# Windowed attention and a squared-relu MLP on one core: the last 512 tokens' first product by seven products, a longer lag of the second product, and a new set of planner constants

## The chip, the core and the metric

The kernel runs on one core of one Trainium2 chip. The metric is device time in microseconds (us). A core has a matrix engine (TensorE, PE in the profile, with its weight loads as PEld), three engines for elementwise work (VectorE is DVE, ScalarE is ACT, GpSimd is POOL) and a synchronisation engine (SP); DMAs are issued from the queues of SP, ACT and POOL. Matrix products land in PSUM, eight banks of 128 partitions x 512 float32; DVE and ACT carry them to SBUF. Each engine works through its own instructions in the order in which they were written, and waits on semaphores for the others.

## The reference, cut to what matters

```python
# q, k, v: (8, 8, 576, 64) = batch, heads, positions, head size; float32
scores = matmul(q, k.T) / sqrt(64)
scores = where(abs(pos_i - pos_j) <= 32, scores, -1e9)      # a band of 65 keys
attn   = softmax(scores)
x = matmul(attn, v), turned to (8*576, 8*64)                # 4608 tokens x 512
h = x @ w_in                                                # 512 -> 2048, "first product"
g = maximum(h, 0) ** 2
out = g @ w_out                                             # 2048 -> 512, "second product"
```

The output is 4608 x 512 float32. The two products are 4608 x 512 x 2048 multiplications each; they run in bf16 with float32 sums.

## The kernel before, in words

**Units.** The 4608 tokens are counted in 72 units of 64. Attention works on 24 groups G of 192 queries (three units, three groups to a batch element, all eight heads at once). The first product works on tiles of 192 tokens up to token 2304 and of 256 tokens after that (`TILES`). The second product works on blocks u of 128 tokens; blocks 0 and 1 are done directly (`mm2`), the others in 17 pairs (`PAIRS`, `mm2_pair`).

**Attention** (`scores_steps` L697, `pv` L753, `xturn`). q and k arrive in rows (`load_qk`, `load_pair`: DMAs on POOL's queue, with a conversion to bf16). They must be turned so that the head size lies on partitions: for groups 0 to 5 (`TG = 6`) by PE transposes (`turn_pe`, L568) and an eviction, later by transposing DMAs on SP's queue (`turn_dma`, L608). PE makes scores, ACT takes exp (L711, L714), DVE multiplies by the band's mask (L719, L725), PE multiplies by v with a column of ones beside it, DVE takes the reciprocal of the sums (L772) and scales (L775) into rows of x, xa (64 tokens) and xb (128 tokens). x must be turned as well: groups below `NXT` do it by PE transposes (L833, L838; group 0 by L808 and L803) and an eviction by ACT (L850), the others by two transposing DMAs on SP's queue (L854, L857) into `XT`.

**First product** (`mm1`, L879). For a tile and each column block of 128 of the 2048 columns, four matmuls with the weight block as the stationary side and the turned x as the moving side. A PSUM bank takes 512 elements (two column blocks of a 256-token tile). ACT takes the relu (L885), and DVE (L893) or ACT (L895) the square, into `GT`, a ring of 24 units.

**Second product** (`mm2_pair`, L965). Two blocks of 128 tokens x 2048 times 2048 x 512 are seen as a 2 x 2 by 2 x 2 block product and made by Winograd's form of Strassen's scheme: seven products where eight are the plain way. DVE forms four sums of `GT` blocks a pair (S1 to S4, L951); sums of the weights are formed once (`setup_tw`, L932). Each of the seven products is eight matmuls of 256 columns. The evictions: P1 goes to SBUF (L976 on ACT or L978 on DVE), DVE adds it to the next (L985: u2, u4, c22, cc), and the last two products accumulate in the bank. Every second pair from block `ULATE` on uses two of attention's banks, which are free by then.

**The order is planned.** Every instruction is recorded with the engine it may run on, a duration from a formula, what it reads and writes, and a key: its place in the work, in units. A list scheduler (`Prog.schedule`) then walks through the time: whenever an engine is free, it takes, of what is ready, the one with the lowest key. What comes out is a fixed order for each engine; nothing is decided on the chip. Attention of group G has the key 3G − `LEAD`, the first product of unit t has t + `MOE` (t − 1), the second product's pair at block u has 2u + `LAGP`. `OFFS` shifts the keys of single kinds of DVE and ACT work (S: the sums of the second product and so on), `FLEX` gives the handicap in units at which a kind may run on its second engine ('g': a square on ACT), `NOISE` and `SEEDS` shift all keys at random. The scheduler also plans the DMAs: a queue, a service time (`QMOVE`, `VMOVE`, `TMOVE`, ...), and then a slack, the time after which the planner counts the data as there: `LSLACK` for loads, `TSLACK` for turned q and k, `XSLACK` for turned rows of x. A load of group G from `GFAR` = 12 on is issued on POOL after a gate, the product with v of group G − 3.

Of the kernel before, what the change touches and what calls it, by code (L numbers as in the profile page):

```python
# [19 lines left out]
RING = 1536  # L20
NV, NRAW = 6, 6
TG = 6
NXT = 3
LEAD = 8
LAG = 9.0
AHEAD = 7
GFAR = 12
GATE = 'P{}B'
GD = 3
GK = 8.0  # L30
TDKEY = 6
XKEY = (0.2, 0.5)
QMOVE = 14.8
HMOVE = 27
PMOVE = 21.5
WMOVE = 86.0
VMOVE = 14.8
TISS = 1340
TMOVE = 12
TGAP = 28  # L40
NVR = 24
VKEY = 10.0
TSLACK = 3500
XSLACK = 2500
LSLACK = 3000
NCLR = 1
LANDQ = 2000
PQ = 100
# [17 lines left out]
SEEDS = (54889, 73113, 37345, 76131, 20885, 97248, 47624, 10448, 1997, 7471, 50773, 3305, 47783, 64133, 39018, 28670, 69087, 23028, 92194, 70005)  # L66
NOISE = 0.0
NBIAS = 1
PKEY = 2
MKEY = (-9.5, -6.5)  # L70
VSET = (-9.8, -6.8)
ESPLIT = 0
SDUR = 541
IOTA = -1
OPENING = [('k', 1), ('w1', 0), ('v', 0, 0), ('q', 1), ('v', 0, 1), ('q', 2), ('w1', 1), ('q', 5),
# [281 lines left out]
class Gen:  # L357
# [103 lines left out]

    def gate(self, G):
        if G < 6:
            return None
        return self.p.named[GATE.format(G - GD)] if G >= GFAR else self.moe

    def load_qk(self, t, b, g, key):
        t0, n = KC[g] if t == "k" else (192 * g, 192)  # L470
        h = n // 2
        G = 3 * b + g
        raw = self.RAW[t][G % NRAW]
        src = (self.q if t == "q" else self.k)[b]
        s = src[:, t0:t0 + n, :].rearrange("h (j p) d -> p j h d", j=2)
        for j in range(2):
            self.p.rec("POOL", lambda e, j=j: e.dma_start(raw[0:h, j, :].rearrange("p (h d) -> p h d", h=8), s[:, j]),  # L477
                       writes=[("raw", t, G % NRAW, j)], dma=(f"{t}{G % NRAW}{j}", G), key=key, dur=500 + 3 * h,
                       move=(h // 2, QMOVE), name=f"{t}{b}{g}{j}", after=self.gate(3 * b + g), slack=LSLACK if b > 1 else 0)

    def load_hw(self, t, g, key):

# [19 lines left out]
    def load_pair(self, t, b, g, key):  # L502

        t0, n = KC[g] if t == "k" else (192 * g, 192)
        h = n // 2
        G = 3 * b + g
        pr, raw = self.PR[t][G % NPR], self.RAW[t][G % NRAW]
        s = (self.q if t == "q" else self.k)[b][:, t0:t0 + n, :].rearrange("h (p r) d -> p h (r d)", r=2)
        self.p.rec("POOL", lambda e: e.dma_start(pr[0:h, :].rearrange("p (h c) -> p h c", c=128), s), writes=[("pr", t, G % NPR)],
                   dma=(f"{t}p{G % NPR}", G), key=key, dur=500 + 3 * h, move=(h // 2, PMOVE), name=f"{t}{b}{g}",  # L510
                   slack=LSLACK1 if b else 0)
        self.p.rec("DVE", lambda e: e.tensor_copy(raw[0:h, :, :].rearrange("p r (h d) -> p r h d", d=64),
                                                  pr[0:h, :].rearrange("p (h r d) -> p r h d", r=2, d=64)),
                   reads=[("pr", t, G % NPR)], writes=[("raw", t, G % NRAW, x) for x in range(2)], key=3 * G - LEAD - PKEY if b == 0 else key, dur=430,
                   name=f"c{t}{b}{g}")

    def load_v(self, b, g, key, js=(0, 1)):
        G = 3 * b + g
        vt = self.V[G % NV]
        for j in js:  # L520
            k0 = 192 * g - 32 + 128 * j
            lo, hi = max(k0, 0), min(k0 + 128, S_)
            if g and j == 0 and G < NVR:
                lo = k0 + 64
            n = hi - lo
            self.p.rec("POOL", lambda e, j=j, lo=lo, hi=hi, k0=k0: e.dma_start(  # L526
                vt[lo - k0:hi - k0, j, :, 0:64], self.v[b, :, lo:hi, :].rearrange("h p d -> p h d")),
                writes=[("v", G % NV, j)], dma=(f"v{G % NV}{j}", G), key=key, dur=500 + 3 * n, move=(n // 2, VMOVE),
                name=f"v{b}{g}{j}", after=self.gate(3 * b + g), slack=LSLACK if b > 1 else LSLACK1 * b)

    def copy_v(self, G, key):
# [86 lines left out]
    def scores(self, G, ws):  # L618
        b, g = divmod(G, 3)
        i = b % 2  # L620
        kt, qt = self.KT[i], self.QT[i]
        key = 3 * G - LEAD + 0.3 * ws[0]
        a = 192 * g
        reg = {w: w if len(ws) == 2 or G < NBIAS else 0 for w in ws}
        if G < NBIAS:
# [57 lines left out]
    def scores_steps(self, G):  # L683
        b, g = divmod(G, 3)
        i = b % 2
        kt, qt = self.KT[i], self.QT[i]
        key = 3 * G - LEAD
        a = 192 * g
        n = G % 2

# [38 lines left out]
    def pv(self, G, w):  # L729
        b, g = divmod(G, 3)  # L730
        n = 2 * G + w
        key = 3 * G - LEAD + 0.3 * w + 0.1
# [55 lines left out]

    def xturn(self, G):
        xa, xb = self.XA[G % 3], self.XB[G % 3]  # L790
        key = 3 * G - LEAD + 0.5
        r = 192 * G % RING
        wr = [("xt", (3 * G + c) % (RING // 64)) for c in range(3)]
        if G < NXT:
            ps = self.AT[:, 1024:1536].bitcast(BF16)
            bank = self.half(2)
# [65 lines left out]
    def mm1(self, t0, n, ds, key):  # L862
# [26 lines left out]
        if SQBEG <= t0 < SQEND and k % SQMOD[1] in SQMOD[0]:  # L889
# [4 lines left out]
                   reads=[("rt", k % 4)], writes=wr, key=key, dur=dve(c), name=f"g{t0}.{d0}",  # L894
                   alt=("ACT", lambda e: e.activation(gt[:, d0:d0 + len(ds), r:r + n], rr, ACTF.Square), act(c), "g")  # L895
                   if "g" in FLEX else None)

    def mm2(self, u, seg, key):
        op, gt = self.OUTP[u % 2], self.GT
# [158 lines left out]
    def build(self):  # L1058
# [40 lines left out]
        for G in range(NG):  # L1099
            b, g = divmod(G, 3)  # L1100
            if b > 1:
                key = 3 * G - LEAD - (GK if G >= GFAR else AHEAD)
                for t in "kq":
                    at(key, self.load_pair if G < TG else self.load_qk, t, b, g, key)
                at(key, self.load_v, b, g, key)
                if g and G < NVR:
                    key = 3 * G - LEAD - 0.5 if G >= VCS else key
                    at(key + 0.01, self.copy_v, G, key - VKEY if G >= VCS else key)
            for t in "kq":
                key = 3 * G - LEAD - (0.6 if G < TG else TDKEY)  # L1110
                at(key, self.turn_pe if G < TG else self.turn_dma, t, b, g, key)
            for ws in ((0,), (1,)) if G < NSPLIT else ():
                at(3 * G - LEAD + 0.3 * ws[0], self.scores, G, ws)
            if G >= NSPLIT:
                at(3 * G - LEAD, self.scores_steps, G)
            for w in range(2):
                at(3 * G - LEAD + 0.3 * w + 0.1, self.pv, G, w)
            at(3 * G - LEAD + 0.5, self.xturn, G)
# [62 lines left out]
```

## Time and profile before

| | |
|---|---|
| time, median of 3 runs | 290.84 us (290.55 to 291.35) |
| the profiled execution: its time, its span | 292.3 us, 290.1 us |
| granted TensorE clock, mean | 0.999 |
| busy: PE, PEld, DVE, ACT, POOL (us) | 283.0, 245.6, 208.2, 206.3, 107.0 |
| matmuls of the first product, L879 | 1248 to ht, 64 to outp, 32 to at |
| DMA, mean over the span | 138 GB/s, 39.97 MB |
| read and written in HBM | 36.70 MB, 9.44 MB |

The span runs from the first to the last instruction of the profiled execution; its time has what lies around it as well. Rows of groups give busy time and the mean of one instruction; a matmul's record is the time from its start to its modelled end, so that neighbours overlap, and how fast a stream of matmuls goes is better read from the chain of waits, which has starts and lengths of runs of them. The line numbers are those of the kernel before.

### The profile page before, as it was taken

What the parts mean: (1) busy time and instruction counts of PE and PEld (TensorE: products, weight loads), DVE (VectorE), ACT (ScalarE), POOL (GpSimd) and SP (SyncE); (2) the same over time, 40 slices, a digit from 0 to 9 for tenths busy, and PEclk for the clock granted to TensorE, in tenths of its full rate; (3) what the DMA queues carried; (4) which work ended last, traced back from release to release, by engine and by line L of the source; (5) the groups of instructions that cost most, each with busy time, mean ns of one, the idle gap of its engine ahead of it and who ended that gap; (6) DMA issues with size and microseconds to landing.
All of it is one profiled execution on the core that took longest, in us unless ns stands there. A gap on an engine that the chain in (4) does not pass through costs nothing.

```text
span 290.1 us, 8378 instructions
## 1 busy us (share of the span) xinstructions
PE 283.0 (98%) x3426; PEld 245.6 (85%) x3430; DVE 208.2 (72%) x451; ACT 206.3 (71%) x379; POOL 107.0 (37%) x143
## 2 busy tenths in 40 slices
PE   7988999999999999999999999999999999999996
PEld 2467885889999999999998898888888888988885
DVE  6668779878687878686968886766876877735263
ACT  3379987586989988778776677758687638688520
POOL 8986660141566066326415435606236000000000
PEclk9999999999999999999999999999999999999999
DMA  9999999999999999999999999999999921202024
GB/s 161 188 194 186 197 178 139 200 135 173 113 143 209 129 165 119 173 171 143 124 150 189 150 127 169 131 190 90 169 106 139 143 91 29 84 18 76 0 75 145
DMA packets 160645, 39.97 MB, mean 138 GB/s; under 512 B 149984, under 2 KB 156256, under 8 KB 160608
## 3 DMA queue, kind: packets, MB, share of 16 engines
q0 software_dynamic: 106016, 17.93, 94.2%
q1 hardware_dynamic: 49552, 12.47, 31.4%
q10 hardware_dynamic: 5040, 9.05, 9.8%
q8 instruction: 27, 0.44, 0.7%
q14 instruction: 10, 0.08, 0.1%
HBM read 36.70 MB, written 9.44 MB: 159 GB/s over the span
## 4 chain that ended last, share of the span: by engine, by line
PE 87%; DVE 6%; ACT 3%; DMA 1%; issue 1%; ACTq 0%; DVEq 0%
PE ht L879 39%; PE outp L965 29%; PE at L965 4%; PE at L753 4%; PE at L697 3%; PE outp L405 2%; DMA oe<-in_q_dram 1%; PE at L879 1%; PE outp L905 1%; PE outp L879 1%; DVE xa L775 1%; DVE tw L932 1%; ACT qt L596 1%; DVE kt L599 1%; ACT e L674 1%
## 5 line engine op out<-in xcount | busy, mean ns | idle before, releaser
L879 PE MATMUL ht<-xt,w 128*128 128x192 bf16 (+1 forms) x1248 | 135.9, 258 | 0.0
L879 PEld LDWEIGHTS ht<-xt,w 128*128 128x128 bf16 x1248 | 109.3, 98 | 7.9 <-ACT qt L596 0.3
L885 ACT ACTIVATE rt<-ht 128x384 bf16<-128x384 f32 (+1 forms) x156 | 82.4, 534 | 36.4 <-PE ht L879 31.4
L477 POOL DMA_DIRECT2D kraw<-in_k_dram x36 | 27.7, 775 | 113.1 <-PE at L753 54.6
L895 ACT ACTIVATE gt<-rt 128x384 bf16<-128x384 bf16 (+1 forms) x116 | 65.3, 569 | 4.4 <-ACT rt L885 1.5
L526 POOL DMA_DIRECT2D v<-in_v_dram x48 | 37.7, 793 | 0.0
L965 PE MATMUL outp<-w,gt 128*128 128x256 bf16 x240 | 31.1, 273 | 0.0
L965 PE MATMUL outp<-tw,gt 128*128 128x256 bf16 x240 | 31.1, 273 | 0.0
L965 PE MATMUL outp<-tw,ss 128*128 128x256 bf16 x240 | 30.5, 273 | 0.3 <-DVE ss L951 0.2
L893 DVE TENSOR_TENSOR gt<-rt 128x384 bf16<-128x384 bf16 (+1 forms) x52 | 19.9, 386 | 13.5 <-ACT rt L885 13.0
L477 POOL DMA_DIRECT2D qraw<-in_q_dram x36 | 27.7, 773 | 0.0
L711 ACT ACTIVATE e<-at 128x1024 bf16<-128x1024 f32 x21 | 21.4, 1020 | 7.3 <-PE at L697 7.0
L965 PEld LDWEIGHTS outp<-tw,ss 128*128 128x128 bf16 x240 | 22.9, 98 | 3.1 <-issue 0.3
L965 PEld LDWEIGHTS outp<-w,gt 128*128 128x128 bf16 x240 | 23.0, 98 | 3.0 <-ACT oe L915 0.5
L965 PEld LDWEIGHTS outp<-tw,gt 128*128 128x128 bf16 x240 | 22.9, 98 | 2.5
L985 DVE TENSOR_TENSOR oe<-outp,uu 128x256 f32<-128x256 f32 (+1 forms) x30 | 16.6, 554 | 8.2 <-ACT rt L885 4.9
L719 DVE TENSOR_TENSOR pt<-e,mask 128x1024 bf16<-128x1024 bf16 x21 | 14.5, 691 | 11.1 <-ACT e L711 11.0
L753 PE MATMUL at<-v,pt 128*128 128x66 bf16 x384 | 20.1, 194 | 0.1
L753 PEld LDWEIGHTS at<-v,pt 128*128 128x128 bf16 x384 | 17.8, 98 | 2.2 <-ACT at L783 0.4
L725 DVE TENSOR_TENSOR pt<-em,mask 64x512 bf16<-64x512 bf16 x42 | 17.6, 420 | 1.7 <-ACT em L714 0.3
L775 DVE TENSOR_TENSOR xa<-at,rs 64x512 bf16<-64x512 f32 x24 | 16.7, 695 | 1.1
L775 DVE TENSOR_TENSOR xb<-at,rs 128x512 bf16<-128x512 f32 x24 | 16.5, 686 | 0.8
(112 smaller groups left out, 321.8 us busy)
## 6 DMA issues: line engine op xcount, KB each, us to landing
out_dram<-oe ACTq DMA_DIRECT2D x34, 256.0 KB, 4.0
qraw<-in_q_dram POOLq DMA_DIRECT2D x36, 96.0 KB, 6.2
w<-in_moe_w_in_dram POOLq DMA_DIRECT2D x4, 512.0 KB, 11.1
v<-in_v_dram POOLq DMA_DIRECT2D x16, 128.0 KB, 7.8
w<-in_moe_w_out_dram POOLq DMA_DIRECT2D x4, 512.0 KB, 17.7
v<-in_v_dram POOLq DMA_DIRECT2D x16, 96.0 KB, 7.0
kraw<-in_k_dram POOLq DMA_DIRECT2D x12, 112.0 KB, 5.5
kraw<-in_k_dram POOLq DMA_DIRECT2D x12, 96.0 KB, 4.4
```

The lines of the kernel that those rows point to most:

```text
L477: self.p.rec("POOL", lambda e, j=j: e.dma_start(raw[0:h, j, :].rearrange("p (h d) -> p h d", h=8), s[:, j]), writes=[("raw", t, G % NRAW, ...
L526: self.p.rec("POOL", lambda e, j=j, lo=lo, hi=hi, k0=k0: e.dma_start(vt[lo - k0:hi - k0, j, :, 0:64], self.v[b, :, lo:hi, :].rearrange("h ...
L711: self.p.rec("ACT", lambda e: e.activation(e2[:], self.AT[:, 0:1024], ACTF.Exp, scale=0.125), reads=lo, writes=[("e", n)], key=key, dur=ac ...
L725: self.p.rec("DVE", lambda e, w=w, r=r, x=x, mm=mm: e.tensor_tensor(pt[x:x + 64, w, :, 0:64], e1[r:r + 64, :].rearrange("p (h q) -> p h q" ...
L753: mm = e.matmul(avp[:, c:c + VS], pt[:, 4 * (h % 2) + h // 2, :], vt[:, w, h, :], start=(w == 0 and y == 0), stop=True, skip_group_check=True)
L775: self.p.rec("DVE", lambda e: e.tensor_tensor(x[r0:128, :].rearrange("p (x y c) -> p x y c", x=2, y=4), av[:, :, :, 0:64], rb, ALU.mult), ...
L879: mm = e.matmul(ht[:, n * x:n * x + n], self.W1[:, ft, 128 * d:128 * d + 128], self.XT[:, ft, r:r + n], start=(ft == 0), stop=(ft == 3))
L885: self.p.rec("ACT", lambda e: e.activation(rt[:, 0:c], ht[:, 0:c], ACTF.Relu), reads=htag, writes=[("rt", k % 4)], key=key, dur=act(c), na ...
L893: self.p.rec("DVE", lambda e: e.tensor_tensor(gt[:, d0:d0 + len(ds), r:r + n], rr, rr, ALU.mult), reads=[("rt", k % 4)], writes=wr, key=ke ...
L895: alt=("ACT", lambda e: e.activation(gt[:, d0:d0 + len(ds), r:r + n], rr, ACTF.Square), act(c), "g")
L965: mm = e.matmul(op[:, 256 * half:256 * half + 256], a[:, d, :], w[:, d, :], start=first and d == 0, stop=d == 7, skip_group_check=True)
L985: self.p.rec("DVE", lambda e: e.tensor_tensor(out, src, other, ALU.add), reads=btags[bank] + rd, writes=wr, key=key + k * PSTEP - DLEAD, d ...
```

## The change

The first product of tokens 4096 to 4607, before two tiles of 256 tokens, is made as one tile of 512 in the manner of the second product: x as 2 x 2 blocks (halves of the 512 features, halves of the 512 tokens), the weights as 2 x 2 blocks (halves of the features, halves of the columns). `setup_w1s` forms four sums of weight blocks on DVE (eight instructions of 1024 elements), `mm1_tile` four differences of x blocks (512 elements), and `mm1_pair` runs, for each of eight pairs of column blocks (dd and dd + 8), seven products of two matmuls of 256 columns, an eviction (p1) and a relu on ACT, four additions on DVE, a relu of the other three quarters (DVE or ACT) and a square of 1024 elements (DVE or ACT). The buffers are those of finished work (raw q and k, `QT`, `KT`, `V`); pairs alternate between the two banks of `HT` and two banks of attention.

All else is constants, and a key of attention that runs ahead by 0.2 units a group after the sixth. `NXT` goes from 3 to 5, so the rows of x of groups 3 and 4 are turned on PE instead of by DMA; `TG` is 6 on both sides. `LAGP` goes from 8 to 14. Slack: `XSLACK` 2500 to 3200, `TSLACK` 3500 to 2200, `LSLACK` 3000 to 1200. The gate of loads is one group earlier.

```diff
-NXT = 3
+NXT = 5
-GK = 8.0
-TDKEY = 6
+GK = 7.0
+TDKEY = 5.0
 QMOVE = 14.8
+QM2 = 21.4
+TBK = 0
+GDL = 1
-TGAP = 28
+TGAP = 16
-TSLACK = 3500
-XSLACK = 2500
-LSLACK = 3000
+TSLACK = 2200
+XSLACK = 3200
+LSLACK = 1200
+STR1 = (4096,)
+LG0 = 6
+LGS = 0.2
+WLEAD = 3
-SEEDS = (54889, ...)
-NOISE = 0.0
+SEEDS = (43876, ...)
+NOISE = 0.1
-PKEY = 2
+PKEY = 0.2
-           ('k', 2), ('v', 1, 0), ('w1', 2), ('v', 1, 1), ('w1', 3), ('q', 3), ('v', 2, 0), ('v', 2, 1),
-           ('k', 3), ('v', 3, 0), ('w2', 2), ('v', 3, 1), ('w2', 0), ('w2', 1), ('hq', 0), ('v', 5, 1),
+           ('k', 2), ('v', 1, 0), ('w1', 2), ('v', 1, 1), ('w1', 3), ('q', 3), ('v', 2, 0), ('v', 3, 1),
+           ('v', 2, 1), ('k', 3), ('v', 3, 0), ('w2', 2), ('w2', 0), ('w2', 1), ('hq', 0), ('v', 5, 1),
-LAGP = 8.0
-PSTEP = 0.4
-SLEAD = 2.5
+LAGP = 14.0
+PSTEP = 0.35
+SLEAD = 1.0
-SQBEG = 768
-ULATE = 28
-HLATE = 4352
+SQBEG = 576
+ULATE = 26
+HLATE = 3840
-OFFS = {'S': 3.25, 'M': -1.5, 'g': 2.25, 'Z': -3.5, 'N': 2.75, 'cc.': -4.25, 'u': -2.75, 'X': 3.25, 'r': -2.25, 'c': -2.25}
+OFFS = {'S': 2.5, 'M': -2.5, 'g': 2.25, 'Z': 3.25, 'N': -1.75, 'cc.': -3.0, 'u': -2.0, 'X': -0.5, 'r': -2.25, 'c': -1.0}
-TWKEY = 6
+TWKEY = 7
-FLEX = {'g': 5.25, 'Z': 4.75, 'ev': 3.0, 'o': 6, 'p': 0.75}
+FLEX = {'g': -1.75, 'Z': -2, 'ev': 0.25, 'o': 4.75, 'p': 3.25, 'm': -1.5}
...
+    def pos(self, G):
+        return 3 * G - LEAD - max(0, G - LG0) * LGS
...
-        return self.p.named[GATE.format(G - GD)] if G >= GFAR else self.moe
+        return self.p.named[GATE.format(G - GD - GDL * (G > LG0))] if G >= GFAR else self.moe
...
-                       move=(h // 2, QMOVE), name=f"{t}{b}{g}{j}", after=self.gate(3 * b + g), slack=LSLACK if b > 1 else 0)
+                       move=(h // 2, QMOVE if b < 2 else QM2), name=f"{t}{b}{g}{j}", after=self.gate(3 * b + g), slack=LSLACK if b > 1 else 0)
...
+    def mm1_pair(self, t0, dd, key):
...
+        L = [w(0, lo), w(1, lo), ws(3), w(1, hi), ws(0), ws(1), ws(2)]
...
+        R = [B[0, 0], B[1, 0], B[1, 1], T[3], T[0], T[1], T[2]]
...
+        prod((0, 5), 0, (0, 1), True, 0, "a")
+        prod((4, 6), 1, (0, 1), True, 1, "b")
+        self.p.rec("ACT", lambda e: e.activation(p1, al[:, 0:256], ACTF.Copy), ...)
...
+        add(u2, al[:, 256:512], p1, btags[0] + tp1[:1], tu2, 1, 256, f"u2.{t0}.{dd}")
+        add(u4, be[:, 0:256], u2, btags[1] + tu2[:1], tu4, 2, 256, f"u4.{t0}.{dd}")
+        add(rh[:, 768:1024], be[:, 256:512], u4, btags[1] + tu4[:1], rtag[2], 3, 256, f"c22.{t0}.{dd}")
+        prod((1,), 0, (0,), False, 4, "c")
+        self.p.rec("ACT", lambda e: e.activation(rh[:, 0:256], al[:, 0:256], ACTF.Relu), ...)
+        prod((2, 3), 1, (0, 1), False, 5, "d")
+        add(rh[:, 256:768]..., be[:, 0:512]..., u2.unsqueeze(1).to_broadcast((128, 2, 256)), ..., 5, 512, f"cc.{t0}.{dd}")
...
+            if t0 in STR1:
+                if t0 == STR1[0]:
+                    at(t0 / 64 - 2.5, self.setup_w1s, t0 / 64 - WLEAD)
+                at(t0 / 64 - 2, self.mm1_tile, t0, t0 / 64 + MOE)
+                for d in range(8):
+                    at(t0 / 64 + d + MOE, self.mm1_pair, t0, d, t0 / 64 + d + MOE)
+                t0 += 512
+                continue
```

More of the change, by code (lines that the diff above doesn't have):

```diff
@@ L513, in load_pair @@
                                                   pr[0:h, :].rearrange("p (h r d) -> p r h d", r=2, d=64)),
-                   reads=[("pr", t, G % NPR)], writes=[("raw", t, G % NRAW, x) for x in range(2)], key=3 * G - LEAD - PKEY if b == 0 else key, dur=430,
+                   reads=[("pr", t, G % NPR)], writes=[("raw", t, G % NRAW, x) for x in range(2)], key=self.pos(G) - PKEY if b == 0 else key, dur=430,
                    name=f"c{t}{b}{g}")
@@ L621, in scores @@
         kt, qt = self.KT[i], self.QT[i]
-        key = 3 * G - LEAD + 0.3 * ws[0]
+        key = self.pos(G) + 0.3 * ws[0]
         a = 192 * g
@@ L686, in scores_steps @@
         kt, qt = self.KT[i], self.QT[i]
-        key = 3 * G - LEAD
+        key = self.pos(G)
         a = 192 * g
@@ L731, in pv @@
         n = 2 * G + w
-        key = 3 * G - LEAD + 0.3 * w + 0.1
+        key = self.pos(G) + 0.3 * w + 0.1
         reg = 1 if NBIAS <= G or G < NDUP and w else 0
@@ L790, in xturn @@
         xa, xb = self.XA[G % 3], self.XB[G % 3]
-        key = 3 * G - LEAD + 0.5
+        key = self.pos(G) + 0.5
         r = 192 * G % RING
@@ L794, in xturn @@
         if G < NXT:
-            ps = self.AT[:, 1024:1536].bitcast(BF16)
-            bank = self.half(2)
+            ps = (self.OUTP[0][:] if 0 < G < TBK else self.AT[:, 1024:1536]).bitcast(BF16)
+            bank = ["outp0"] if 0 < G < TBK else self.half(2)
             two = G < NBIAS
@@ L1101, in build @@
             if b > 1:
-                key = 3 * G - LEAD - (GK if G >= GFAR else AHEAD)
+                key = self.pos(G) - (GK if G >= GFAR else AHEAD)
                 for t in "kq":
```

102 lines of the change are left out of this document (94 added, 8 removed).

## The prediction

> **What bounds the kernel now.** I read the page's shares and slices first, then the busy time by stretches, then the chain of waits, and last single rows of the timeline. The page's first rows (engine: busy us, share of the span, instructions) and the shares of the chain:
>
> ```profile
> span 290.1 us, 8378 instructions
> PE 283.0 (98%) x3426; PEld 245.6 (85%) x3430; DVE 208.2 (72%) x451; ACT 206.3 (71%) x379; POOL 107.0 (37%) x143
> ...
> PE 87%; DVE 6%; ACT 3%; DMA 1%; issue 1%; ACTq 0%; DVEq 0%
> ```
>
> The chain that ends last runs on TensorE for 87% of the span. The same by stretches (start:end, length, then busy us and count for PE, weight loads, DVE, ACT, POOL; granted clock, DMA share, GB/s):
>
> ```profile
> 20.00:70.00 50.00, 48.43 (x649) 40.71 (x651) 40.17 (x84) 39.94 (x76) 20.11 (x27) 1.00 1.81 176
> 45.00:244.00 199.00, 198.45 (x2515) 177.21 (x2515) 152.98 (x316) 148.97 (x280) 73.66 (x96) 1.00 1.59 144
> 70.00:280.00 210.00, 209.92 (x2567) 189.66 (x2566) 151.60 (x315) 156.96 (x293) 69.24 (x90) 1.00 1.31 126
> 243.00:287.00 44.00, 44.00 (x436) 39.31 (x434) 22.58 (x46) 25.85 (x46) 0.00 (x0) 1.00 0.16 53
> ```
>
> From 70 to 280 us PE idles 0.08 us of 210 at full clock: there a PE instruction removed is time won, and one added is time lost. Before 70 us there are 1.57 us of idle time between 20 and 70, and the work before 20. In the last 44 us DVE is busy 22.58 and ACT 25.85: half of each is free. The profiled execution took 292.3 us, 2.2 more than its span, and 1.5 more than the median of the runs, 290.84; I add differences of the span to 290.84.
>
> **First part: seven products for tokens 4096 to 4607.** Before, two tiles of 256 tokens, 16 column blocks and four matmuls each make 128 matmuls of 256 columns. After, eight pairs of seven products of two matmuls make 112 of the same shape. Chain rows of the end (start, us, what):
>
> ```profile
> 264.63 0.87 PE at L879 x8
> ...
> 268.12 0.87 PE ht L879 x8
> ```
>
> Eight take 0.87 us, so one 0.109: 16 fewer are **−1.75 us**, all on the full engine.
>
> In exchange DVE gets additions. The rows that price them (busy us, mean ns):
>
> ```profile
> L879 PEld LDWEIGHTS ht<-xt,w 128*128 128x128 bf16 x1248 | 109.3, 98 | 7.9 <-ACT qt L596 0.3
> ...
> L895 ACT ACTIVATE gt<-rt 128x512 bf16<-128x512 bf16 x48 | 30.3, 630 | 2.5 <-ACT rt L885 1.0
> ...
> L711 ACT ACTIVATE e<-at 128x1024 bf16<-128x1024 f32 x21 | 21.4, 1020 | 7.3 <-PE at L697 7.0
> ...
> L985 DVE TENSOR_TENSOR uu<-outp,uu 128x256 f32<-128x256 f32 x30 | 12.6, 421 | 3.1 <-ACT uu L976 1.5 <-PE outp L965 0.5
> ...
> L985 DVE TENSOR_TENSOR oe<-outp,uu 128x512 f32<-128x512 f32 x15 | 10.4, 691 | 8.0 <-ACT rt L885 4.9 <-PE outp L965 2.9
> ...
> L951 DVE TENSOR_TENSOR ss<-gt 128x1024 bf16<-128x1024 bf16 x15 | 10.3, 689 | 3.0 <-ACT gt L895 2.4 <-PE outp L965 0.2
> ...
> L893 DVE TENSOR_TENSOR gt<-rt 128x512 bf16<-128x512 bf16 x24 | 10.1, 424 | 7.6 <-ACT rt L885 7.3
> ...
> L533 DVE COPY v<-v 64x512 bf16<-64x512 bf16 x16 | 6.1, 383 | 1.7 <-PE ht L879 1.2
> ...
> L976 ACT ACTIVATE uu<-outp 128x256 f32<-128x256 f32 x9 | 3.4, 382 | 2.0 <-PE outp L965 1.8
> ...
> L932 DVE TENSOR_TENSOR tw<-w 128x1024 bf16<-128x1024 bf16 x4 | 2.7, 687 | 0.1
> ...
> L512 DVE COPY qraw<-tw 96x1024 bf16<-96x1024 bf16 x5 | 2.4, 472 | 0.1
> ...
> L850 ACT ACTIVATE xt<-at 128x768 bf16<-128x768 bf16 x2 | 1.6, 811 | 0.1
> ```
>
> Sums of weights (ws): 8 x 0.69 = 5.5 us of DVE once; differences of x (t0 to t3): 4 x 0.42 = 1.7. A pair has three adds of 256 (1.26), one of 512 (0.69), one square of 1024 (0.69) and one relu of 768 in bf16, for which no row stands: a copy of 512 took 0.38 and one of 1024 0.47, so it lies between, and I take 0.42. That is 3.06 on DVE, 24.5 for eight, and 2 x 0.38 on ACT. What they replace is 16 relus of 0.60 on ACT and 16 squares of 0.42 (DVE) or 0.63 (ACT).
>
> Is that hidden? A pair of the second product is 56 matmuls, 6.1 us of PE, and on DVE four sums of 0.69 and the additions 3 x 0.42 + 0.69: 4.7 us. With a lag of 14 units the tile (key 63) still has the pairs u = 26 to 34 behind it: 5 x 6.1 + 112 x 0.109 = 42.8 us of PE. DVE has 24.5 + 1.7 + 5 x 4.7 = 49.7 us if nothing moves. But squares (0.69 each, 5.5) and relus (0.42 each, 3.4) may go to ACT, and the change lowers their handicap there (g from 5.25 to −1.75, m −1.5); before, with the handicap, ACT took 48 of the 72 squares of 512 elements (L895 against L893). All moved, DVE has 40.8 us and ACT 13 pairs x 0.76 + 8 x (1.1 + 0.81) = 25; the square of 1024 on ACT has no row, it lies between one exp of 1.02 and two squares of 1.26. The sums of pairs 26 and 28 (5.5 us) can run before the tile begins, and so can the 5.5 of ws, since attention ends earlier. That leaves 35 to 41 of 42.8: covered, with little to spare. A pair holds its two banks for some 3.7 us (eight matmuls 0.88, the eviction 0.38, three adds 1.26, four matmuls 0.44, an add 0.69), then come relu and square; the second set of banks and the second products between are the cover of that, and the pairs 28 and 30 stand between the last square and the first product that needs it. With the cover gone it costs up to 6.9 (49.7 − 42.8). Range 0 to +6.9, **I take +0.3**, since the engine idles for half of this stretch now.
>
> **Second part: two more groups' x rows turned on PE.** NXT goes from 3 to 5, so groups 3 and 4 leave the transposing DMA. (TG, the q and k turned on PE, is 6 on both sides.) PE timeline at the two turns of before, and SP's queue at the third group:
>
> ```profile
> 26.58 0.29 PE L833 MATMUL at<-ident,xa 64*128 64x64 bf16 x4 [0.61 <-DVE xb L775]
> 26.80 0.40 PE L838 MATMUL at<-ident,xb 128*128 128x128 bf16 x4
> 27.03 0.82 PE L879 MATMUL ht<-xt,w 128*128 128x192 bf16 x8
> ...
> 33.93 0.29 PE L833 MATMUL at<-ident,xa 64*128 64x64 bf16 x4
> 34.15 0.40 PE L838 MATMUL at<-ident,xb 128*128 128x128 bf16 x4
> 34.39 0.82 PE L879 MATMUL ht<-xt,w 128*128 128x192 bf16 x8
> ```
>
> A turn holds PE 0.45 us; two are **+0.9**, and 2 x 0.81 on ACT. It takes four transposes off SP, which are then not ahead of kt and qt in that queue.
>
> On transposes the Trainium skill speaks against this part. "TensorE: Matmul & The Clock Gate", section Part 4: PE-mode transpose, gives about 275 ns for one in a kernel's context. Sixteen would be 4.4 us and the sum 3.5 higher; the rows, eight in 0.45 us at clock 1.00, disagree, and I go by them.
>
> **Third part: the order.** Lag 14 for 8, attention earlier by 0.2 units a group after the sixth, other offsets, handicaps and random shifts: no instruction is added, and in 70 to 280 us there are 0.08 us to win. (TBK at 0 and SQBEG change nothing that runs; ULATE and HLATE put pair 26 and the tiles from 3840 on attention's free banks.) The planned slack for loads (3000 to 1200) and for kt and qt (3500 to 2200) falls, x's rises (2500 to 3200). If these are too small PE waits in order, with mm1 and mm2 queued behind it. But the gate now opens a group earlier (four groups ahead for three) and attention's lead over mm1 grows from 7 to 10.4 units, so the data lie ready longer; cost 0. In the opening the idle 1.57 us and the start are open. Timeline from the last attention step of group 0 to the first product:
>
> ```profile
> 15.91 0.21 DVE L772 RECIPROCAL rs<-at 128x8 f32<-128x8 f32 x1 [0.29 <-PE at L753]
> ...
> 16.15 0.42 DVE L512 COPY qraw<-tw 96x1024 bf16<-96x1024 bf16 x1
> ...
> 16.49 0.68 DVE L775 TENSOR_TENSOR xb<-at,rs 128x512 bf16<-128x512 f32 x1
> ...
> 17.66 0.28 PE L803 MATMUL ht<-ident,xb 128*128 128x128 bf16 x2
> ...
> 17.77 1.02 ACT L674 ACTIVATE e<-at 128x1024 bf16<-128x1024 f32 x1 [0.49 <-PE at L649]
> ...
> 18.69 0.38 ACT L822 ACTIVATE xt<-ht 128x256 bf16<-128x256 bf16 x1
> ...
> 19.18 0.83 PE L879 MATMUL ht<-xt,w 128*128 128x192 bf16 x8
> ```
>
> A cast of q (L512) stands ahead of xb and holds it 0.4 us; PKEY 2 to 0.2 puts such casts later. The eviction of xt waits for an exp that began at 17.77. So the first product can come up to 0.4 + 0.7 earlier or, reordered for the worse, as much later; with the idle time the term goes from −2.7 to +1.1. I take **−0.9**.
>
> Sum: −1.75 + 0.3 + 0.9 − 0.9 = −1.45, so 290.84 − 1.45 = **289.4 us**.
>
> **Rivals.** 0.3% of 290.84 is 0.9 us, about what a measurement of this kernel tells from no change: faster is below 289.97, slower above 291.71.
>
> More is won: the opening gives its whole 2.7 and the tail nothing lost, 290.84 − 1.75 + 0.9 − 2.7 = 287.3, with most of it some 288. Against it: it needs every idle moment before 70 us. The Trainium skill would expect more here: "Perfetto Trace Analysis", section Identifying the Most-Contended Engine, judges TensorE's headroom by weight loads, busy 85% here; a tenth of the rest would be 4.4 us and the sum 285.0. The rows disagree: weight loads of 98 ns under matmuls of 109 can't pass 90%.
>
> No change: the opening wins nothing, PE pays the two turns, −1.75 + 0.9 + 0.3 = −0.55, 290.3. For it: PE runs second products without idling while x is late.
>
> Slower, DVE becomes the bound of the tail: from key 63 on, DVE's queue holds sums, adds, relus and squares in one order, and a late add holds a bank and PE with it. No stretch of ten us in the trace has DVE above this:
>
> ```profile
> 40.00:50.00 10.00, 9.79 (x119) 6.44 (x119) 8.78 (x20) 7.56 (x13) 3.12 (x5) 1.00 2.10 154
> ```
>
> At 0.88, 40.8 us take 46.4: +3.6 in place of +0.3, −1.75 + 0.9 − 0.9 + 3.6 = +1.85, 292.7. It decides once fewer than about half of the 16 movable operations go to ACT, or the sums of 26 and 28 come late. Against it: half of DVE and ACT is free there now.
>
> Slower, the loads can't follow: a unit of 64 tokens is 1.5 us of second product (6.1 / 4) and 1.75 of first (16 matmuls), so the longer lag (6 x 1.5) and the lead (3.4 x 3.3) want the last scores some 20 us sooner, and the bytes of 45 to 244 us at 144 x 199 / 179 = 160 GB/s. The stretch from 20 to 70 moved 176. If they don't come, second products are used up before the tile, and its additions alone set its pace: 24.5 less half of what may move (4.4) is 20.1 us for 12.2 of PE; at half such a shortfall +3.9, so 293.3. Rows on both (last scores; POOL's waits in all, times, longest):
>
> ```profile
> 244.28 0.52 PE L697 MATMUL at<-qt,kt 64*128 64x64 bf16 x24
> ```
>
> ```profile
> POOL kraw L477 <- PE at L753: 54.6, 8, 14.1
> ```
>
> POOL stood 54.6 us at such gates with nothing to load, so there is room.
>
> **Chances and range.** Forecast 0.42 (its own range 288.5 to 289.95), more 0.13, no change 0.24, DVE tail 0.14, loads 0.07. That the change doesn't do what it says (fewer matmuls don't show) I count as nil: the counts follow from the code. Faster 0.55, same 0.24, slower 0.21. The range reaches over most of "more" and half of the DVE tail: 287.6 to 292.3.
>
> **What would show it.** Right: 16 fewer matmuls of the first product, a PE stretch from 70 us to the end as full as now, a first product before 19.2 us, DVE near 85 to 95% in the last 43 us with most squares on ACT. Wrong: PE idle in the last 45 us released by DVE lines of the new pair (tail), PE waiting on kt or qt transposes after 70 us (loads), or an opening that ends later than now.

## The result and the profile after

The changed kernel takes 288.81 us (median; 288.3 to 291.74), the kernel before, measured beside it, 290.56 us (290.2 to 292.42): a ratio of 0.9942, 95% interval [0.9927, 0.9957], so 1.7 us faster (1.2 to 2.1). The forecast was 289.4, 1.45 us faster. Ratios and intervals, here and below, are of executions in the chip's fast state alone; only three executions, all of one experiment (the three parts), fell in its slower state.

The profiled execution of the changed kernel tells less of this than one would wish: it took 291.74 us, the longest of all its runs, with a span of 289.9 us, while all others had spans of 286.5 to 288.4. Some 2 us of the difference are a longer opening, which the last section shows and which the profile before has as well, and 1.2 us are the two waits below. It is read here for what was where, and the times are taken from the runs. The page's rows that answer to those of before:

```profile
span 289.9 us, 8460 instructions
PE 282.1 (97%) x3424; PEld 245.2 (85%) x3430; DVE 219.8 (76%) x472; ACT 215.4 (74%) x404; POOL 106.8 (37%) x143
...
PE 87%; DMA 5%; DVE 5%; ACT 2%; issue 1%; DVEq 0%
```

DVE has 11.6 us more work than before, ACT 9.1, and the chain that ends last still runs on PE for 87% of the span. By stretches (length, then busy us of PE, weight loads, DVE, ACT, POOL):

```profile
20.00:70.00 50.00, 48.92 (x676) 42.13 (x678) 39.84 (x82) 47.27 (x94) 24.72 (x33) 1.00 1.83 174
...
70.00:280.00 210.00, 208.67 (x2543) 187.88 (x2541) 163.72 (x339) 158.52 (x298) 64.49 (x84) 1.00 1.25 125
...
243.00:287.00 44.00, 44.00 (x405) 39.28 (x402) 34.33 (x72) 21.80 (x39) 0.00 (x0) 1.00 0.16 59
...
270.00:280.00 10.00, 10.00 (x94) 8.95 (x93) 9.04 (x18) 1.07 (x2) 0.00 (x0) 1.00 0.29 105
```

Three things are to be seen. In the last 44 us PE is full, as before, though DVE has gone from 22.58 to 34.33 us there; the work that the seven products put on DVE and ACT is hidden. In the last complete ten us DVE is busy 9.04 beside a full PE. And between 70 and 280 us PE has 1.33 us of idle time where before had 0.08; the waits of PE name it (us in total, times, longest):

```profile
PE ht L889 <- DMA xt<-xb: 0.7, 1, 0.7
...
PE at L763 <- DVE pt L735: 0.5, 1, 0.5
```

A turned row of x came late once, and a mask product once. How the new tile lies on PE is in the chain of waits (start, us, what; L966 are the new products, L1083 the second products):

```profile
265.09 0.44 PE ht L966 x4
265.52 0.22 PE at L966 x2
265.74 0.87 PE outp L1083 x8
266.62 0.87 PE at L1083 x8
267.49 0.44 PE at L966 x4
267.93 1.75 PE outp L1083 x16
269.67 3.49 PE at L1083 x32
```

Second products stand between the new ones, and after the last of the new ones come 176 matmuls of second products. 112 of those are the pairs 32 and 34, which need the tile; the other 64 (7.0 us) are older, and they are what PE does while the last square is made. Some of the groups of the new work on DVE and ACT in the last 44 us (count, busy us, mean ns):

```profile
L993 DVE TENSOR_TENSOR kt<-ht,kt 128x256 f32<-128x256 f32 x8 | 3.4, 423 | 0.9 <-PE ht L966 0.8
...
L993 DVE TENSOR_TENSOR v<-ht,kt 128x512 bf16<-128x512 f32 x4 | 2.8, 692 | 0.5 <-PE ht L966 0.5
```

```profile
L1014 ACT ACTIVATE gt<-v 128x1024 bf16<-128x1024 bf16 x8 | 8.4, 1054 | 0.1
L1008 ACT ACTIVATE v<-v 128x768 bf16<-128x768 bf16 x8 | 6.7, 836 | 0.5 <-DVE v L993 0.5
```

All eight squares and all eight relus run on ACT, at 1.05 and 0.84 us.

### The profile page after: what moved, and what is told of

Read it like the earlier page. It is cut to its first block, busy times and chain, and to the rows that moved or that the text cites. A ratio compares the mean times of both kernels' runs of the same rounds, so it can differ in the third digit from the quotient of the medians.

```text
span 289.9 us, 8460 instructions
## 1 busy us (share of the span) xinstructions
PE 282.1 (97%) x3424; PEld 245.2 (85%) x3430; DVE 219.8 (76%) x472; ACT 215.4 (74%) x404; POOL 106.8 (37%) x143
## 4 chain that ended last, share of the span: by engine, by line
PE 87%; DMA 5%; DVE 5%; ACT 2%; issue 1%; DVEq 0%
PE ht L889 32%; PE outp L1083 29%; PE at L1083 6%; PE at L763 4%; DMA xt<-xb 3%; PE at L707 3%; PE outp L1023 2%; PE at L966 2%; PE ht L966 2%; DMA oe<-in_q_dram 1%; PE outp L412 1%; PE outp L889 1%; PE at L889 1%; DVE kt L609 1%; PE at L578 1%
## 5 line engine op out<-in xcount | busy, mean ns | idle before, releaser
L889 PE MATMUL ht<-xt,w 128*128 128x192 bf16 (+1 forms) x1120 | 119.5, 256 | 0.7 <-DMA xt<-xb 0.7
L889 PEld LDWEIGHTS ht<-xt,w 128*128 128x128 bf16 x1120 | 96.6, 98 | 8.0 <-DMA xt<-xb 1.0
L895 ACT ACTIVATE rt<-ht 128x384 bf16<-128x384 f32 (+1 forms) x140 | 72.2, 529 | 21.7 <-PE ht L889 20.6
L905 ACT ACTIVATE gt<-rt 128x384 bf16<-128x384 bf16 (+1 forms) x122 | 67.1, 566 | 2.4
L1083 PE MATMUL outp<-w,gt 128*128 128x256 bf16 x224 | 29.0, 273 | 0.0
L1083 PE MATMUL outp<-tw,gt 128*128 128x256 bf16 x224 | 29.0, 273 | 0.0
L1083 PE MATMUL outp<-tw,ss 128*128 128x256 bf16 x224 | 28.9, 273 | 0.1
L1083 PEld LDWEIGHTS outp<-w,gt 128*128 128x128 bf16 x224 | 21.5, 98 | 2.6
L1083 PEld LDWEIGHTS outp<-tw,gt 128*128 128x128 bf16 x224 | 21.7, 98 | 2.3
L1083 PEld LDWEIGHTS outp<-tw,ss 128*128 128x128 bf16 x224 | 21.2, 98 | 2.7 <-DVE ss L1069 0.3
L903 DVE TENSOR_TENSOR gt<-rt 128x384 bf16<-128x384 bf16 (+1 forms) x30 | 11.4, 382 | 10.2 <-ACT rt L895 10.0
```

The costliest lines, as they stand in the source:

```text
L889: mm = e.matmul(ht[:, n * x:n * x + n], self.W1[:, ft, 128 * d:128 * d + 128], self.XT[:, ft, r:r + n], start=(ft == 0), stop=(ft == 3))
L895: self.p.rec("ACT", lambda e: e.activation(rt[:, 0:c], ht[:, 0:c], ACTF.Relu), reads=htag, writes=[("rt", k % 4)], key=key, dur=act(c), na ...
L1083: mm = e.matmul(op[:, 256 * half:256 * half + 256], a[:, d, :], w[:, d, :], start=first and d == 0, stop=d == 7, skip_group_check=True)
```

## The experiments

All constants not named are those of the kernel that the experiment starts from, and except for the two that repeat an instruction in place, the whole order is planned anew; that is the limit of what each shows. The changed kernel's constants, its random shifts among them, go with its own order, so an order that is planned anew may also be worse by chance. Comparisons with the change are made by the ratios to before, which was measured beside each.

**Without the seven products.**

```diff
-STR1 = (4096,)
+STR1 = ()
```

> The changed kernel with the last 512 tokens made by the plain product again; all constants, the turns, the lag and the attention lead stay as changed. Theory of the prediction (16 matmuls of 0.109 us on a full TensorE are the gain, the tail costs nothing): 1.75 us slower than the changed kernel, so 290.6 us, level with the kernel before (ratio 0.998 to 1.002). Rival, the new order is the gain and the seven products pay for themselves at best: 288.8 us, ratio about 0.994. Rival, DVE holds the tail up and eats part of the gain: faster than the changed kernel, under 288.5. In the profile the waits of PE for turned rows of x near 159 and for a mask product near 181 us should be there again if they belong to the order, and gone if they were one execution's chance.

290.97 us, ratio to before 1.0003 [0.998, 1.0026]. The seven products are worth 0.9942 to 1.0003, 0.6% or 1.8 us (about 0.8 either way), and everything else in the change together is worth nothing that can be seen (by its interval from 0.6 us faster to 0.8 slower). The 16 matmuls come to 1.75. The two waits of the profile above are not in this one: from 140 to 220 us, where both lay, PE is full.

```profile
70.00:140.00 70.00, 69.84 (x977) 64.77 (x975) 53.38 (x112) 56.88 (x119) 36.20 (x48) 1.00 1.72 164
140.00:220.00 80.00, 80.00 (x994) 70.64 (x992) 60.81 (x127) 64.73 (x116) 28.33 (x37) 1.00 1.62 145
```

That alone would not separate the order from the execution, for the order is a new one here. The two experiments below that keep the changed kernel's order do: PE idles 0.62 and 0.48 us there between 70 and 280 us, where the profile above has 1.33. In one of them the same matmul waits for the same turned row again (0.51 us at 159.29); the wait for the mask's product is in neither. So about 0.5 us belong to the order, and the rest to that execution.

**The seven products alone, on before's constants.**

```diff
 # before's constants and keys
+STR1 = (4096,)
```

> The kernel before, with its own constants (lag 8, attention not running ahead, three x turns on TensorE), and only the last 512 tokens by seven products. Theory: the products need the second products that the longer lag leaves behind them. With lag 8 four pairs are left (u = 28 to 34) and two of these wait for the tile, while DVE has 24.5 + 1.7 + 5.5 of sums and additions for 12.2 us of PE in it: 3 to 8 us slower than before, PE idle in the last 45 us released by DVE lines of the new pair. Rival, fewer matmuls win by themselves: 289.1 us, 1.75 faster than before. Rival, neutral: 290.6.

298.24 us, 1.0248 [1.0206, 1.029]: 7.2 us slower. PE idles in the tile, first for the additions (DVE L993) and then, 2.9 us at a stretch, for the last square (ACT L1014):

```profile
PE outp L1083 <- ACT gt L1014: 2.9, 1, 2.9
PE at L966 <- DVE v L993: 2.5, 4, 0.9
```

```profile
260.00:270.00 10.00, 8.28 (x71) 6.20 (x68) 9.50 (x23) 6.46 (x15) 0.00 (x0) 1.00 0.15 56
270.00:280.00 10.00, 5.62 (x45) 3.82 (x46) 8.28 (x19) 7.99 (x13) 0.00 (x0) 1.00 0.00 0
```

When the tile began, at 258.5 us, 120 matmuls of second products were left, 112 of them in need of the tile. The changed kernel had 272 left when its tile began at 245.1 (matmuls of L1083 that start later in the trace, here and below).

**The shorter lag.**

```diff
-LAGP = 14.0
+LAGP = 8.0
```

> The changed kernel with the second product 8 units behind instead of 14, all else as changed. Theory: with 8 the pairs that cover the tile are used up before it; 3 to 7 us slower than the changed kernel (292 to 296), with PE idle in the last 45 us. Rival, the lag is only a matter of priority and PE fills itself anyway: within 0.5 us of 288.8.

297.03 us, 1.0209 [1.017, 1.0247]: some 8 us slower than the change, a little more than expected. 208 matmuls of second products are left when the tile begins and 112 when it ends, so nothing covers the last square. PE's timeline there:

```profile
273.53 0.39 PE L966 MATMUL at<-xt,kraw 128*128 128x256 bf16 x2 [1.23 <-DVE v L993]
273.75 0.38 PE L966 MATMUL at<-qt,w 128*128 128x256 bf16 x2
277.45 1.86 PE L1083 MATMUL outp<-w,gt 128*128 128x256 bf16 x8 [3.31 <-ACT gt L1014]
```

The last of these rows holds more than its wait. Its eight matmuls take 1.86 us, where eight of their kind take 1.04 elsewhere in these traces: the granted clock has fallen to 0.50 from 276 to 280 us, which over ten us looks like this (0.75 is the mean clock):

```profile
270.00:280.00 10.00, 5.46 (x39) 3.91 (x37) 7.03 (x14) 3.99 (x7) 0.00 (x0) 0.75 0.14 52
```

21 matmuls follow each other at 0.21 us in place of 0.109 before the clock is full again, 2.1 us on top of the 3.31 of the wait. All four kernels here whose PE stood idle for 2.3 us or more in the tail show it (14 to 21 matmuls at half the pace, 1.4 to 2.1 us); the changed kernel has no such matmul there. A tail without cover therefore costs more than its idle time.

**Attention not running ahead.**

```diff
-LG0 = 6
+LG0 = 99
```

> The changed kernel without the key that lets attention run ahead by 0.2 units a group (and so also with the load gate at three groups for all). Theory of the prediction: the lead is not needed for the middle, where nothing waits, but the tile wants attention's banks and DVE free: 0 to 3 us slower than the changed kernel, 289 to 292 us, and last scores later than 226 us. Rival, the lead is what gives the tile its cover: as slow as the shorter lag, 295 us or more, with PE idle in the tile.

299.8 us, 1.0326 [1.0306, 1.0346]: 11 us slower than the change, and the rival was right. The gate of the loads goes back with the lead, and the two are not separated. The last scores move from 226.9 to 241.6 us and the tile from 245.1 to 258.0 (in a profile whose first product started 1.7 us earlier), and in the meantime PE has done second products: 136 are left at the tile's start, 112 at its end. The waits are those of the two kernels above:

```profile
PE outp L1083 <- ACT gt L1014: 2.9, 1, 2.9
PE at L966 <- DVE v L993: 1.7, 3, 0.9
```

So the lag is only a wish. The planner gives PE whatever is ready, and a long lag comes about only if attention is early enough for first products to be ready instead of second ones. The lag is needed as well. Second products left at the tile's start: 272 with lead and lag, 208 with the lead and a lag of 8, 136 with the lag of 14 and no lead, and 120 with neither, on before's constants.

**Squares and relus kept on DVE.**

```diff
-                   alt=("ACT", lambda e: e.activation(x, x, ACTF.Relu), act(768), "m"))
+                   alt=None)
...
-                   alt=("ACT", lambda e: e.activation(out, src, ACTF.Square), act(1024), "g"))
+                   alt=None)
```

> The changed kernel with the relu of three quarters and the square of the eight new pairs kept on DVE (ACT may not take them). Theory: DVE then has some 49.7 us of work for the 42.8 us that PE needs from the first new product on, less what the sums of pairs 26 and 28 do before: 2 to 7 us slower than the changed kernel (291 to 296), DVE 95% busy or more in the stretch that holds PE up. Rival, DVE has room: within 0.5 us of 288.8.

295.82 us, 1.0159 [1.0113, 1.0204]: by the ratios 6.3 us slower than the change, about 1.4 either way, the upper part of what was expected. PE waits in the tile for DVE, once for an addition of the new pairs and once for a sum of the second product (L1069):

```profile
PE at L1083 <- DVE qraw L1069: 2.3, 1, 2.3
...
PE at L966 <- DVE v L993: 1.2, 1, 1.2
```

```profile
270.00:280.00 10.00, 6.49 (x46) 4.81 (x44) 9.23 (x19) 1.32 (x4) 0.00 (x0) 0.83 0.14 52
```

DVE is at 9.23 of 10 and PE down to 6.49; from 266 to 276 us, around these waits, DVE is at 9.70, the 95% that was expected. The two waits and 1.4 us lost to matmuls at the lowered clock make some 5 us in the tail. In this profile a turned row of x held PE 2.1 us as well, before the tile, so that its span is no measure of the tail by itself.

**More DVE work in the same order.**

```diff
+                if name.startswith("c22"):
+                    e.tensor_tensor(<unused half of V 4 or 5>, src, other, ALU.add)
                 return e.tensor_tensor(out, src, other, ALU.add)
```

> The changed kernel in the same order, with one more addition on DVE in each of the eight new pairs (the c22 add is issued once more, ahead of itself, into an unused place): 8 x 0.42 = 3.4 us of DVE. In the profile of the changed kernel DVE idles some 5 us between 240 and 270 us while PE is full. Theory, covered with little to spare: 0 to 2 us slower than the changed kernel, 288.8 to 290.8. Rival, DVE already sets the pace of the tail: the whole 3.4 us, 292.2. Rival, ample cover: 288.8, no change.

289.02 us, 0.995 [0.9923, 0.9978], beside 0.9942 for the change: no difference that can be told, 0.2 us by the ratios and at most about 1 of the 3.4. The tail has cover to spare as long as ACT shares the work:

```profile
250.00:260.00 10.00, 10.00 (x93) 8.72 (x92) 9.37 (x23) 8.51 (x16) 0.00 (x0) 1.00 0.14 54
```

DVE is at 9.37 of 10 with PE full beside it.

**The turns of groups 3 and 4 issued twice, in the same order.**

```diff
             def f0(e):
-                for j in range(4):
+                for j in (0, 1, 2, 3) * (1 + (G > 2)):
...
             def f1(e):
-                for j in range(4):
+                for j in (0, 1, 2, 3) * (1 + (G > 2)):
```

> The changed kernel in the same order, with the sixteen transposes of groups 3 and 4 issued twice (the second set writes the same values), so that what a turn costs on TensorE is measured by itself. Theory: every instruction on TensorE there is on the path, 0.45 us a turn: 0.9 us slower than the changed kernel, ratio to before near 0.997. Rival, the turns lie in idle time of the opening: 0 to 0.3 us, ratio about 0.994 to 0.995. By the longer price for a transpose (275 ns each) it would be 4.4 us, ratio above 1.009.

289.17 us, 0.9965 [0.994, 0.999]: by the ratios 0.7 us over the change, but about 0.8 either way, so that the times alone don't tell it from nothing. PE's timeline gives the price (the doubled transposes, and the next instruction):

```profile
42.18 0.40 PE L843 MATMUL at<-ident,xa 64*128 64x64 bf16 x8
42.52 0.62 PE L848 MATMUL at<-ident,xb 128*128 128x128 bf16 x8
42.97 0.51 PE L578 MATMUL at<-ident,qraw 96*128 96x96 bf16 x8
```

0.79 us from 42.18 to 42.97, where a single turn took 0.45 before and 0.46 at the same place in the changed kernel: eight transposes more are some 0.34, two turns 0.7.

**Three x turns again.**

```diff
-NXT = 5
+NXT = 3
```

> The changed kernel with three groups' x turned on TensorE as before (groups 3 and 4 by the transposing DMA again). Theory: TensorE gets 0.9 us back, and part of the opening's gain of 0.9 is lost since x comes later: between 0.9 faster and 0.5 slower than the changed kernel, 287.9 to 289.3 us. Rival, the early turns are what lets the first product run ahead in the opening: 1 to 3 us slower than the changed kernel, with PE waiting for turned x or running out of work between 40 and 70 us.

292.73 us, 1.0078 [1.0065, 1.0091]: 3.9 us slower than the change, more even than the rival's 1 to 3. The tail is as full as in the change: the last scores come at 227.9 us, and 272 second products are left when the tile begins. PE idles early, 2.26 us between 20 and 70 and 2.35 between 70 and 140:

```profile
20.00:70.00 50.00, 47.74 (x632) 39.97 (x633) 39.55 (x85) 38.74 (x77) 21.24 (x29) 1.00 1.80 176
70.00:140.00 70.00, 67.65 (x942) 62.99 (x941) 50.41 (x109) 58.26 (x123) 34.58 (x45) 1.00 1.75 155
```

That PE would run out of work early was the rival's sign, but a wait for turned x, its other one, is not among PE's waits. The longest after 20 us are for a relu on ACT (1.0 us, at 81), for the loads of weights (0.8), for an exp (0.6), and one of 1.2 us before scores at 86.5 that the profile gives no releaser for. So the run shows that this order without the two turns is 3.9 us worse; it does not show by what way the turns help.

**Five x turns alone, on before's constants.**

```diff
-NXT = 3
+NXT = 5
```

> The kernel before with the rows of x of groups 3 and 4 turned on TensorE, and nothing else of the change. Theory: two turns of 0.45 us on a busy TensorE less the idle time that they can fill: 0.3 to 0.9 us slower than before (290.8 to 291.4). Rival, earlier rows of x help this order as well: faster than before, 289.5 to 290. Rival, the planned order shifts for the worse: over 291.5.

292.57 us, 1.005 [1.0026, 1.0074]: 1.5 us slower than before, 0.8 to 2.1. More than the 0.9 of the two turns, though not surely so. By themselves, then, the turns cost, and out of the changed kernel they can't be taken without a loss. Which of the change's other parts makes the difference, or whether the planned order without them is only an unlucky one, isn't shown.

**Three parts on before's constants: products, lag 14, attention ahead.**

```diff
 # before's constants, and
+STR1 = (4096,)
-LAGP = 8.0
+LAGP = 14.0
+LG0, LGS, GDL = 6, 0.2, 1
```

> The kernel before with three things of the change and no other: the seven products, the lag of 14, and attention running ahead with the earlier gate; three x turns on TensorE, and before's slack, offsets, handicaps and no random shifts. Theory: what the tail needs is there, so it is at least level with before and up to 1.75 us faster (289.0 to 290.8). Rival, the other constants (handicaps that move squares to ACT, above all) are needed too: 2 us or more slower than before.

292.59 us, 1.0064 [1.0042, 1.0086]: some 2 us slower than before by the ratio. The ratio goes by nine executions of 290.64 to 294.1 us; three more took 296.2 to 296.3. The time is about the rival's, but its reason isn't what the profile shows: with before's handicaps all eight squares and all eight relus of the new pairs are on ACT as well, 272 second products are left when the tile begins, and the tail is full. The time goes earlier:

```profile
70.00:140.00 70.00, 68.23 (x980) 63.47 (x977) 51.10 (x109) 62.57 (x131) 38.66 (x51) 1.00 1.86 157
...
250.00:260.00 10.00, 10.00 (x94) 8.98 (x92) 8.38 (x19) 8.10 (x16) 0.00 (x0) 1.00 0.15 55
```

1.77 us of PE idle between 70 and 140, and ACT at 62.57 of 70; the longest of these waits is for a relu on ACT (0.86 us).

**The same with five turns and the change's slack.**

```diff
 # the three, and
-NXT = 3
+NXT = 5
-TSLACK, XSLACK, LSLACK = 3500, 2500, 3000
+TSLACK, XSLACK, LSLACK = 2200, 3200, 1200
```

> The kernel before with the seven products, lag 14 and the lead of attention, and now also the five x turns on TensorE and the change's three slacks; offsets, handicaps, opening and random shifts as before. With the three alone PE stood idle 1.8 us between 70 and 140 us and runs spread over 5.6 us. Theory: the turns and the slack are what was missing there: 289.0 to 290.5 us, faster than with the three, PE idle under 0.5 us from 70 to 140 us, runs within 2 us of each other. Rival, offsets and random shifts are needed for it: 291.5 us or more.

290.55 us, 0.9991 [0.9967, 1.0014]; 290.05 to 292.47. Two us of the three parts' loss are back (2.1, about 0.9 either way), the time is at the upper end of what was expected and the spread, 2.4 us, a little over it; the nine executions that count above spread over 3.5. In the profile PE idles 0.39 us between 70 and 140:

```profile
70.00:140.00 70.00, 69.61 (x963) 64.56 (x964) 54.09 (x117) 57.43 (x118) 32.43 (x42) 1.00 1.82 156
```

Turns and slack were added together, so their shares are not told apart. The 1.4 us that are still missing to the change (about 0.8 either way) must lie with what was left as before: offsets, handicaps, opening, random shifts and the smaller keys and marks of the diff; which of them wasn't tried.

**Less slack for rows of x.**

```diff
-XSLACK = 3200
+XSLACK = 2500
```

> The changed kernel with the slack planned for turned rows of x at 2500 as before, instead of 3200, and the order that comes of it. Theory: attention runs far enough ahead, so the slack is worth nothing: within 0.7 us of the changed kernel, 288.1 to 289.5 us. Rival, turned rows come later than 2500 allows, and PE waits for them in order: 1 us or more slower, with more waits of the first product for xt in the profile than the one of 0.7 us that the changed kernel showed, and a wider spread of the single runs.

289.29 us, 0.9952 [0.9926, 0.9978]; 288.83 to 291.11. Not to be told from the change, and its profile shows no wait of PE for turned x. The larger slack isn't shown to do anything in this order.

## Why the prediction was right, and where its steps were not

**Fewer matmuls, −1.75: right.** Taking the products out costs 1.8 us, about 0.8 either way. This is the gain of the change.

**The tail, +0.3: right that it is covered.** PE is full to the end, and 0.3 us is too little to be told from nothing. The work that may move all moved, ACT doing squares at 1.05 us (estimated 1.1) and relus at 0.84 (0.81); a relu that stays on DVE takes 0.35 (taken as 0.42). The lowered handicaps, which the prediction gave as the reason, aren't needed for that: with before's handicaps all sixteen moved as well. DVE is busy 34.33 of the last 44 us, 78%, and not the 85 to 95 that were to be the sign. With none moved the loss is 6.3 us where the bound was 6.9, but only some 5 of these are seen in the tail, 1.4 of them from the lower clock, which the bound didn't have. Too cautious was the rival's step that DVE can't be denser than 0.88, taken from the densest ten us of before: that was demand and not capacity; 0.90 to 0.94 was seen with PE full, and of 3.4 us more work at most about 1 shows.

**The third part, "cost 0" for the order: right as a sum, the mechanism only half seen.** The whole of the order and the turns is worth nothing that can be seen. But the forecast took the lead of attention as a move that costs nothing and gains little ("the data lie ready longer"), and the pairs 26 to 34 behind the tile as a thing that the lag of 14 brings about. Without the lead 136 second products were left at the tile and not 272, and the time was 11 us worse. The rival on loads did name the condition, that the last scores must come some 20 us sooner or the second products are used up before the tile; it put 3.9 us on half of such a shortfall, so 7.9 on all of it, and the clock that falls after the wait was not in that. Counting what is ready shows why: PE isn't idle, so a second product waits only if a first one can be done in its place. The size of the cover was right where lead and lag are there, 5 pairs or 280 matmuls forecast and 272 found.

**Two turns, +0.9: the price about right, the role missed.** A doubled set of transposes costs 0.34 us a turn beside the 0.45 of a whole one with its changes of kind, and nothing like 275 ns each, so the trace's rows were the better guide than the figure of the Trainium skill ("TensorE: Matmul & The Clock Gate", Part 4: PE-mode transpose). But I counted the turns as a cost alone. Without them the changed kernel is 3.9 us slower, and PE idles 4.6 us between 20 and 140 us in the profile. They are not what gives the tile its cover, for that is 272 without them too; what they do for the order before 140 us stays open.

**The opening, −0.9: not there, and the sum came right by luck.** In the two profiled executions the first product starts at 19.18 before and 19.36 after; in the shorter opening of the last section it starts at 17.2 us in the two experiments on before's constants that had it and at 17.35 to 17.7 in those on the change's. Moving the casts back brought nothing. Idle time between 20 and 70 us went from 1.57 to 1.08. All parts but the seven products come to 0.0 us by the run without them, which is what +0.9 and −0.9 make together; that they were right as a sum and not one by one is luck. By the pieces it would be some 0.7 for the turns, 0.5 of idle time won between 20 and 70 us and about 0.5 lost after 70; the interval of the zero, about 0.8 either way, is too wide to settle it.

**Loads.** That they can follow was right: the last scores start 17.7 us earlier (226.9 for 244.6; 20 were estimated), and no wait for q, k or v appears on PE.

**A rival's reading.** Against more gain the prediction said that weight loads can't pass 90% under matmuls of 109 ns. That holds for tiles of 256 tokens (8.95 of 10 us with PE full). With tiles of 192, between 70 and 140 us of before, weight loads were busy 65.72 of 70 us, 94%. That there was no room left there stays true, since PE idled 0.00 of these 70 us.

## What to carry to other kernels

On a full engine a change is worth the instructions that it takes away, if the work that it hands to other engines has something to hide behind; count that cover as instructions that are ready at that point, not as keys or lags that ask for it. A lag behind a producer comes about only when the producer is early, so that what feeds it (here attention and its loads) has to be moved with it. A step that costs when made alone can be missed when it is taken out of the whole: make the parts alone and also take them out one at a time, and look in the trace whether the way was the one you thought. Where PE stands idle for 2.3 us or more, as in these tails, look at the granted clock behind the wait too.

## What the runs showed of the hardware that wasn't expected

The opening comes in two lengths. The kernel issues matmuls on a tile of zeros (`zz`, L412) where PE has no work yet. In some profiles matmuls run at half the pace until some point between 9.6 and 10.4 us, in others only until one between 4 and 6. PE's timeline of the changed kernel:

```profile
6.44 3.19 PE L412 MATMUL outp<-zz 128*128 128x512 bf16 x7
9.42 0.82 PE L578 MATMUL outp<-ident,kraw 112*128 112x112 bf16 x8
```

and of the one without the seven products, whose instructions on PE are in the same order there:

```profile
5.81 1.68 PE L412 MATMUL outp<-zz 128*128 128x512 bf16 x7
7.66 0.55 PE L578 MATMUL outp<-ident,kraw 112*128 112x112 bf16 x8 [0.17 <-DVE v L406]
```

The seven matmuls of zeros start 0.43 us apart in the first (2.98 us to the next instruction) and 0.22 apart in the second (1.68 us with the end of the last), where PE then even waits 0.17 us. k's rows had been cast by 8.17 us in the first, so PE was late with the turn of k only because the matmuls of zeros stood ahead of it. From there the whole kernel is shifted: the first product starts at 19.36 and 17.35 us. The rows of granted clock show 1.00 in both, so here the distance of the starts is what to look at. The Trainium skill's page "TensorE: Matmul & The Clock Gate", Part 1: The HAM clock gate, says that the clock is halved until a free-running window of about 3.4 us has been found busy, and that where the window falls differs from run to run; distances of 0.43 and 0.22 us and a change of pace that comes at another time in each profile agree with that; the length of the window no run here shows. Both kernels' profiled executions had the long opening, so they can be compared with each other, and less well with the experiments, of which all but two (the turns alone, and the three parts with five turns and slack) had the short one.
